# Threshold attention followed by hash routing: three start-up and routing steps moved to other places in the instruction streams

## The chip, the cores and the metric

The kernel runs on one core of a Trainium2 chip. The metric is the device time of one execution in microseconds. Before the change the median of three runs is 1003.69 us (1003.37 to 1003.96). The profile below is of one more execution, whose span is 1001.3 us.

The core has five engines that work in parallel, each through its own stream of instructions: TensorE (PE in the profile; its weight loads are PEld), VectorE (DVE), ScalarE (ACT), GpSimd (POOL) and SyncE (SP), which issues most of the DMAs.

## The reference, cut to what matters

```python
# attention: batch 8, 8 heads, 576 positions, head_dim 64
scores = (1 / np.sqrt(64)) * np.matmul(q, k.transpose(0, 1, 3, 2))
thresh = np.max(scores, axis=-1, keepdims=True) - tau
scores = np.where(scores >= thresh, scores, -1e9)
scores = scores - np.max(scores, axis=-1, keepdims=True)
attn = np.exp(scores)
attn = attn / (np.sum(attn, axis=-1, keepdims=True) + 1e-9)
x = np.matmul(attn, v)                       # (8, 8, 576, 64) -> x of (4608, 512)

# routing: 8 experts of 512 x 1024 and 1024 x 512
expert_idx = token_ids * np.int64(2654435761) % np.int64(8)
for e in range(8):
    mask = expert_idx == e
    out[mask] = np.maximum(x[mask] @ w1[e], 0.0) @ w2[e]
```

The expert of a token depends on its id alone, not on the attention. So the routing tables (which token goes to which slot of which expert) can be made while the attention runs. Each expert has 608 slots; tokens beyond that would go to an overflow list of 128-row tiles, worked off in a loop at the very end.

## The kernel before: the parts that the change touches

The attention goes over 32 pairs of heads `p`, each in five steps `s` (a step of 64 queries, then four of 128), so `n = 5 * p + s`. Step 0 has one tile of scores, the other four have two. The four operations that every tile of scores passes on its way:

```python
def score(n, j):      # PE: q times k into one of two PSUM tiles "sc"                 (line 219)
def negate(n, j):     # DVE: ns = -sc, with the row minimum; frees "sc"               (line 230)
    # behind a step's last tile, on POOL: thr = row minimum + drop                    (line 237)
def expo(n, j):       # ACT: w = exp(row minimum - ns)                                (line 244)
def mask(n, j):       # DVE: w = w * (ns <= thr), with the row sum                    (line 255)
```

Then PE transposes `w` (line 266), ACT copies the transposes out of PSUM (line 287), and PE multiplies by v (line 297). One pair later the output is normalised by DVE (`put_xm`, line 336).

The start, where tau and the identity matrix come in:

```python
load_pair(0)
...                                        # token ids, v of pair 0
load_pair(1)
make_identity(nc, ident[:])                # POOL: memset, then a select on the diagonal
none_f = a_st.tile([P, 1], FP32, name="none_f")
...                                        # memsets on DVE
with tc.manual_schedule():                 # from here in this order on every engine
    tr = ps_tr.tile([P, 2, 512], FP32, name="tr")
    for _ in range(16):
        nc.tensor.transpose(tr[:, 0, 0:P], ident[:], ident[:])      # nobody reads these
    nc.gpsimd.dma_start(out=tau_in[:], in_=...)
    nc.vector.tensor_scalar(out=keep_any[:], in0=tau_in[:], ..., op0=ALU.is_ge)
    nc.vector.tensor_scalar(out=drop[:], in0=keep_any[:], ...)
    nc.vector.tensor_tensor(out=drop[:], in0=drop[:], in1=tau_in[:], op=ALU.max)
    nc.vector.tensor_scalar(out=k_scale[:], in0=keep_any[:], ...)
    nc.vector.tensor_scalar(out=kts[0][:, 0], in0=kts[0][:, 0], scalar1=k_scale[:], ...)
    nc.scalar.activation(kts[0][:, 1], kts[0][:, 1], AF.Copy, scale=k_scale[:])
    constants()                            # iotas, memsets, triangular matrix, on POOL
    next(pieces)
    score(0, 0)
```

Routing is a generator, `route()`, cut by `yield` into pieces of at most two small DVE operations. Each `next(pieces)` puts one piece into the streams. With the calls counted from the one just above, the pieces hold:

```python
# call 3: eid, eidf            5: onehot                7, 9: two halves of a scan (incl)
# call 10: row                12: two matmuls (L407, L408) and cnt
# call 13: ot_i, twice        14: ot                   15: oend, base         16: base
# call 17: incl + base        19: incl * onehot        21: reduce to rank_f   22: rank_i
# call 23: rank_i, twice      24: rank                 25: ovt, first         26: ovt
# call 27: ovt, twice         28: first                29: slot_i, then placed.append(True)
# call 31: overflow compare   33: overflow reduce      34: min                35: two copies (ov_i)
# the calls not named (2, 4, 6, 8, 11, 18, 20, 30, 32) only reach the next yield
```

Once `placed` is set, a second generator, `scatters()`, runs one piece in each step but step 1: 36 indirect DMAs on POOL, one pair later 16 table loads on SP, one pair later two small DVE operations. From pair 26, step 2, `fetch_0` gathers rows by these tables and needs them done.

The order inside a step, cut to what matters here:

```python
for n in range(LAST + NS + 1):
    p, s = divmod(n, NS)
    ...
    if s == 3 and n < LAST:
        next(pieces, None)                 # ahead of negate(n, 0)
    ...
    if s == 1 and p + 1 < NP:
        scale_k(p + 1)                     # POOL: k of the next pair times keep_any * 0.125
    ...                                    # turns, products with v
    if n < LAST and s not in (1, 2):       # (in steps 1 and 2 this comes a little earlier)
        negate(n, 0); expo(n, 0)
    if s == 0 and n < LAST:
        next(pieces, None)                 # behind negate(n, 0), ahead of put_xm and mask
    if s == 0 and p >= 2 and n != LAST:
        put_xm(p - 2)
    ...
    score(n + 1, 0)
    negate(n, 1); expo(n, 1)
    score(n + 1, 1)
    ...
    for j in range(heads(n - 1)):
        mask(n - 1, j)
    if s != 1 and placed:
        next(scatter_pieces, None)
```

Behind this loop the tables for the experts are made (`stok`, `gidx`, `gidx_x`, on DVE), the last rows are gathered, and the first expert's matmuls go on (`fill`, line 579, each result copied out of PSUM by DVE, line 586).

Of the kernel before, what the change touches and what calls it, by code (L numbers as in the profile page):

```python
# [9 lines left out]
FP32 = mybir.dt.float32  # L10
# [4 lines left out]
ALU = mybir.AluOpType  # L15
# [5 lines left out]
def kernel(  # L21
# [12 lines left out]
    nc = tc.nc  # L34
# [51 lines left out]
    slot_i = consts.tile([P, NTC], I32, name="slot_i")  # L86
    tid32 = consts.tile([P, NTC, 2], I32, name="tid32")
    tau_in = consts.tile([P, 1], FP32, name="tau_in")
    keep_any = consts.tile([P, 1], FP32, name="keep_any")
    k_scale = consts.tile([P, 1], FP32, name="k_scale")  # L90
    drop = consts.tile([P, 1], FP32, name="drop")

# [35 lines left out]
    with tc.tile_pool(name="a_q", bufs=1) as a_q, \  # L128
# [67 lines left out]
                nc.sync.dma_start(out=v_sb[half, 4, half], in_=rows[TAIL:S, half])  # L196

        def scale_k(p):
            nc.gpsimd.tensor_scalar(out=kts[p][:], in0=kts[p][:], scalar1=keep_any[:],
                                    scalar2=SCALE, op0=ALU.mult, op1=ALU.mult)  # L200

        def heads(n):
            return 1 if n % NS == 0 else 2
# [314 lines left out]
                                      offset=0, ap=[[2 * NTC, P], [2, NTC], [1, 2]]))  # L518
        load_v(0)
        load_pair(1)  # L520
        make_identity(nc, ident[:])
        none_f = a_st.tile([P, 1], FP32, name="none_f")
        nc.vector.memset(none_f[:], 0.0)
        for w in w_bufs:
# [9 lines left out]
        def constants():  # L534

            nc.gpsimd.iota(iota_i[:], pattern=[[1, NOV]], base=0, channel_multiplier=0)
            nc.gpsimd.tensor_copy(iota_f[:], iota_i[:])
            make_upper_triangular(nc, u128[:], val=1.0, diag=False)
            nc.gpsimd.memset(ones128[:], 1.0)
            nc.gpsimd.memset(none[:], BIG)  # L540
            nc.gpsimd.memset(gidx[:], BIG)
            nc.gpsimd.memset(gidx_x[:], BIG)
            for t in sidx:
                nc.gpsimd.memset(t[:], BIG)
            nc.gpsimd.iota(tok[:], pattern=[[1, NTC]], base=0, channel_multiplier=NTC)
            for table in slot_dram:
                nc.sync.dma_start(out=table.rearrange("(p c) o -> p (c o)", p=P), in_=none[:])
# [69 lines left out]
                next(h_pieces, None)  # L617

        with tc.manual_schedule():

            tr = ps_tr.tile([P, 2, 512], FP32, name="tr")
            for _ in range(16):
                nc.tensor.transpose(tr[:, 0, 0:P], ident[:], ident[:])
            nc.gpsimd.dma_start(out=tau_in[:],
                                in_=bass.AP(tensor=tau.tensor, offset=0, ap=[[0, P], [1, 1]]))

            nc.vector.tensor_scalar(out=keep_any[:], in0=tau_in[:], scalar1=0.0, scalar2=None,
                                    op0=ALU.is_ge)  # L630
            nc.vector.tensor_scalar(out=drop[:], in0=keep_any[:], scalar1=-3e38, scalar2=3e38,
                                    op0=ALU.mult, op1=ALU.add)
            nc.vector.tensor_tensor(out=drop[:], in0=drop[:], in1=tau_in[:], op=ALU.max)
            nc.vector.tensor_scalar(out=k_scale[:], in0=keep_any[:], scalar1=SCALE, scalar2=None,
                                    op0=ALU.mult)
            nc.vector.tensor_scalar(out=kts[0][:, 0], in0=kts[0][:, 0], scalar1=k_scale[:],
                                    scalar2=None, op0=ALU.mult)
            nc.scalar.activation(kts[0][:, 1], kts[0][:, 1], AF.Copy, scale=k_scale[:])
            constants()
            next(pieces)  # L640
            score(0, 0)
            for n in range(LAST + NS + 1):
                p, s = divmod(n, NS)
                m = n - 2
                if s == 0 and p + 2 < NP:
                    load_pair(p + 2)
                if s == 0 and p + 1 < NP:
                    load_v(p + 1)
                if s == 2 and p in (20, 24):
                    load_w1(p // 4 - 5)  # L650
                if s == 2 and p in (22, 26):
                    load_w2((p - 22) // 4)

                if s == 3 and n < LAST:
                    next(pieces, None)
                if s == 1 and 3 <= p < 2 + KT:
                    nc.sync.dma_start(out=xg_bufs[p - 2][:], in_=xg_bufs[0][:])

                if s == 1 and 2 + KT <= p < 2 + KT + N // DIN:
                    r0 = DIN * (p - 2 - KT)  # L660
                    nc.sync.dma_start(
                        out=x_dram[r0:r0 + DIN, DIN - P:].rearrange("(t p) m -> p t m", p=P),
                        in_=xg_bufs[0][:].rearrange("p (t m) -> p t m", m=P))
                q = p - 1
                if s == 1 and 0 <= q < NP:
                    add_eps(q)
                if s == 1 and p + 1 < NP:
                    scale_k(p + 1)
                if s == 2 and 0 <= q < NP:
                    nc.vector.reciprocal(recs[q][:], recs[q][:])  # L670
                if n == LAST + NS:
                    fill(2)
                if s == 0 and p >= 2:
                    turn_o()
                if n == LAST:
                    for k in (0, 2):
                        tr = ps_sc.tile([P, 2, 512], FP32, name="sc")
                        early_xT(tr, k, k + 2, 0, CO - 1)
                if s in (1, 2) and 0 <= q < NP and n != LAST + 1:
                    av_part(q, 0, ((0, 1, 2), (3, 4))[s - 1])  # L680
                if n < LAST and s in (1, 2):
                    negate(n, 0)
                    expo(n, 0)
                if s == 2 and 0 <= q < NP:
                    put_oT(0)
                if n > LAST:
                    fill(1)
                turned = 0 <= m < LAST
                if turned:
                    tr = turn_w(m, 0)  # L690
                    put_wT(m, 0, tr)
                if n == LAST:
                    put_xm(p - 2)
                    av_part(q, 0, (0, 1, 2))
                if n >= LAST:
                    fill(1)
                if n == LAST:
                    tr = ps_sc.tile([P, 2, 512], FP32, name="sc")
                    early_xT(tr, 4, 5, 0, CO - 1)
                if s in (3, 4) and 0 <= q < NP:  # L700
                    av_part(q, 1, ((0, 1, 2), (3, 4))[s - 3])
                if n < LAST and s not in (1, 2):
                    negate(n, 0)
                    expo(n, 0)
                if s == 0 and n < LAST:
                    next(pieces, None)
                if s == 0 and p >= 2 and n != LAST:
                    put_xm(p - 2)
                if s == 4 and 0 <= q < NP:
                    put_oT(1)  # L710
                if s in (3, 4) and turned:
                    tr = turn_w(m, 1)
                if n + 1 < LAST:
                    score(n + 1, 0)
                if s == 4 and turned:
                    put_wT(m, 1, tr)
                if n < LAST and heads(n) == 2:
                    negate(n, 1)
                    expo(n, 1)
                if s == 3 and turned:  # L720
                    put_wT(m, 1, tr)
                if n + 1 < LAST:
                    score(n + 1, 1)
                if s in (0, 1) and turned:
                    tr = turn_w(m, 1)
                    put_wT(m, 1, tr)
                if 0 < n <= LAST:
# [6 lines that stand above are left out]
                if n >= G0 and s > 1 and early:  # L734
                    assert routed
                    fetch_0(*early.pop(0))
                if n == LAST:
                    fill(1)
            assert not early
            nc.vector.tensor_tensor(out=stok[:], in0=stok[:], in1=stok_odd[:], op=ALU.min)  # L740
            for h in range(4):
                rows, n = slice(32 * h, 32 * h + 32), (NB - h + 3) // 4
                nc.vector.tensor_copy(gidx[rows, :, 0:n], stok[rows, :, h::4])
            for g in range(4):
                rows, n = slice(32 * g, 32 * g + 32), min(KT, NB - KT * g)
                nc.vector.tensor_copy(gidx_x[rows, 1:, 0:n], stok[rows, 1:, KT * g:KT * g + n])
            for kt in range(KT):
                fetch_0(kt, HP - 1)
            fill(FO * 2 * (CO - 1) - 18)
            tr = ps_tr.tile([P, 2, 512], FP32, name="tr")  # L750
            early_xT(tr, 0, KT, CO - 1, CO)
# [195 lines left out]
```

## Time and profile before

| engine | busy us | share of the span |
|---|---|---|
| PE | 983.8 | 98% |
| DVE | 517.7 | 52% |
| ACT | 436.9 | 44% |
| POOL | 291.7 | 29% |

The shares are averages over two stages. In the attention (to about 455 us) PE and DVE are both busy nine tenths of the time or more; in the experts' stage (from about 475 us) PE alone is. A pair takes about 13.9 us in the steady part of the attention.

The start, in the order of the trace: POOL writes zeros for the identity at 0.90 us, issues tau's DMA at 1.48 us (0.74 us of POOL's time), and makes the diagonal at 2.32 us. PE's 16 transposes run from 2.69 us; the last starts at 5.95 us. DVE starts `keep_any` at 4.65 us, which ends a wait of 1.41 us for tau's transfer, the two operations of `drop` at 4.83 and 5.02 us, `k_scale` at 5.10 us, and the first scaling of k at 5.28 us. The first scores start at 6.30 us, the first `negate` at 7.60 us.

In the lists by group, "x32" is the number of instructions, and the number behind the comma is the mean duration of one in ns. In the timeline, the first two columns are the start and the duration in us; what stands in brackets is the idle time of the engine before the instruction and what ended it.

### The profile page before, as it was taken

The page shows a single profiled execution, that of the slowest core. Times are in us where ns is not written, and L with a number is a line of the kernel's source. Part 1 is how long each engine was busy: PE and PEld are TensorE (multiplying, and loading weights), DVE is VectorE, ACT ScalarE, POOL GpSimd, SP SyncE. Part 2 cuts the span into 40 slices and gives each one's busy share as a digit, 9 for nine tenths or more (in the row PEclk, how much of TensorE's full clock was granted, in tenths as well). Part 3 has the DMA queues.
Part 4 walks back from the last instruction along what each step waited for, and adds up shares of the span by engine and source line. Part 5 has one row for each costly group of instructions (what it writes and reads, how often), then busy time and mean ns, then how long its engine had stood idle before and what let it go on. Part 6 is the DMA issues. An engine that isn't in the chain of part 4 may idle for free.

```text
span 1001.3 us, 20487 instructions
## 1 busy us (share of the span) xinstructions
PE 983.8 (98%) x7562; PEld 653.9 (65%) x7562; DVE 517.7 (52%) x1378; ACT 436.9 (44%) x714; POOL 291.7 (29%) x413
## 2 busy tenths in 40 slices
PE   7999999999999999999999999999999999999995
PEld 4666666666666666666766857768578577685773
DVE  7999999999999999994311010010101100200000
ACT  5988888888988889883200000010010000100000
POOL 3233323377676335550321030030210300300101
PEclk9999999999999999999999999999999999999998
DMA  7355544564467677410166344272352533801001
GB/s 182 74 129 141 129 117 112 136 141 107 92 185 169 154 195 194 114 49 25 39 189 185 116 105 143 91 211 89 106 163 84 158 91 104 222 1 39 27 10 57
DMA packets 145779, 117.07 MB, mean 117 GB/s; under 512 B 59860, under 2 KB 120280, under 8 KB 145680
## 3 DMA queue, kind: packets, MB, share of 16 engines
q1 hardware_dynamic: 135408, 96.41, 37.9%
q0 software_dynamic: 7824, 18.91, 6.1%
q8 instruction: 61, 1.00, 0.4%
q10 hardware_dynamic: 2448, 0.44, 0.2%
q14 instruction: 38, 0.31, 0.1%
HBM read 81.99 MB, written 22.37 MB: 104 GB/s over the span
## 4 chain that ended last, share of the span: by engine, by line
PE 87%; issue 6%; SPq 2%; DMA 2%; ACT 1%; DVE 1%; POOL 0%; POOLq 0%; ACTq 0%
PE sc L784 20%; PE av L297 17%; PE sc L219 15%; PE o_ps L802 12%; PE tr L266 10%; PE sc L815 8%; PE sc L579 3%; SPq L835 2%; PE av L266 1%; DMA out_dram<-o_last,gidx 1%; DMA out_dram<-o,gidx 1%; ACT w L244 1%; PE xT_ps L596 0%; PE sc L596 0%; ACT wT_a L287 0%
## 5 line engine op out<-in xcount | busy, mean ns | idle before, releaser
L244 ACT ACTIVATE w<-ns,nmx 128x576 f32<-128x576 f32 x288 | 220.3, 776 | 33.2 <-DVE ns L230 33.1
L784 PE MATMUL sc<-xT,w_sb 128*128 128x304 f32 x896 | 230.4, 419 | 0.0
L255 DVE SCALAR_TENSOR_TENSOR w<-ns,thr,w 128x576 f32<-128x576 f32 x288 | 225.4, 814 | 0.4 <-POOL thr L237 0.4
L784 PEld LDWEIGHTS sc<-xT,w_sb 128*128 128x128 f32 x896 | 170.2, 190 | 61.4 <-issue 3.3
L230 DVE TENSOR_SCALAR_CACHE_REDUCE ns<-sc 128x576 f32<-128x576 f32 x288 | 205.2, 744 | 6.3 <-PE sc L219 5.6
L219 PE MATMUL sc<-k_sb,q 64*128 64x288 f32 (+1 forms) x1280 | 179.2, 426 | 0.6 <-DVE ns L230 0.4
L802 PE MATMUL o_ps<-w_sb,h 128*128 128x512 f32 (+2 forms) x400 | 166.2, 575 | 0.0
L266 PEld LDWEIGHTS tr<-ident,w 64*128 64x128 f32 x2624 | 106.6, 139 | 88.7 <-ACT wT_b L287 26.3
L237 POOL TENSOR_SCALAR thr<-nmx,drop 128x2 f32<-128x2 f32 (+1 forms) x160 | 101.8, 637 | 176.7 <-DVE ns L230 163.4
L792 DVE TENSOR_SCALAR h<-sc 128x608 f32<-128x608 f32 x28 | 22.2, 791 | 240.9 <-PE sc L784 240.9
L266 PE MATMUL tr<-ident,w 64*128 64x64 f32 x2624 | 139.3, 231 | 2.7 <-ACT wT_a L287 2.0
L804 ACT COPY o<-o_ps 128x512 f32<-128x512 f32 (+2 forms) x25 | 14.2, 569 | 274.5 <-PE o_ps L802 248.1
L802 PEld LDWEIGHTS o_ps<-w_sb,h 128*128 128x128 f32 x400 | 74.9, 190 | 86.8 <-issue 84.7
L841 POOL DMA_INDIRECT out_dram<-o,gidx x24 | 23.9, 996 | 324.0 <-ACT o L804 291.4
L219 PEld LDWEIGHTS sc<-k_sb,q 64*128 64x128 f32 (+1 forms) x1280 | 93.0, 179 | 22.9 <-DVE ns L230 9.7
L297 PE MATMUL av<-wT_a,v 128*64 128x320 f32 (+1 forms) x704 | 100.4, 418 | 0.0
L790 ACT ACTIVATE h<-sc 128x608 f32<-128x608 f32 x28 | 19.0, 677 | 182.0 <-PE sc L784 182.0
L815 PE MATMUL sc<-h,w_sb 128*128 128x224 f32 x512 | 98.2, 352 | 0.0
L815 PEld LDWEIGHTS sc<-h,w_sb 128*128 128x128 f32 x512 | 96.9, 190 | 1.1
L287 ACT COPY wT_a<-tr 128x512 f32<-128x512 f32 (+1 forms) x128 | 81.7, 638 | 20.7 <-PE tr L266 20.1
L287 ACT COPY wT_b<-tr 128x512 f32<-128x512 f32 (+1 forms) x128 | 81.2, 634 | 6.4 <-PE tr L266 4.0
L297 PE MATMUL av<-wT_b,v 128*64 128x256 f32 x640 | 83.2, 389 | 0.0
(118 smaller groups left out, 547.9 us busy)
## 6 DMA issues: line engine op xcount, KB each, us to landing
w_sb<-in_moe_w_dram SPq DMA_DIRECT2D x16, 2048.0 KB
q<-in_q_dram SPq DMA_DIRECT2D x62, 288.0 KB
v<-in_v_dram SPq DMA_DIRECT2D x32, 256.0 KB
x_scratch<-xm SPq DMA_DIRECT2D x32, 256.0 KB
xT<-xq SPq DMA_DIRECT2D x84, 80.0 KB
k_sb<-in_k_dram SPq DMA_DIRECT2D x31, 144.0 KB
k_sb<-in_k_dram SPq DMA_DIRECT2D x32, 112.0 KB
o_last<-oq SPq DMA_DIRECT2D x210, 16.0 KB
```

The lines of the kernel that those rows point to most:

```text
L219: nc.tensor.matmul(sc[out_rows, i, 0:S2], lhsT=q_sb[rows, h, q0:q1], rhs=k_sb[rows, h], start=True, stop=True)
L230: nc.vector.tensor_scalar(out=ns[:].rearrange("p (i s) -> p i s", i=2), in0=sc[:, :, 0:S2], scalar1=-1.0, scalar2=None, op0=ALU.mult, op1= ...
L237: nc.gpsimd.tensor_scalar(out=thr[:, 0:j + 1], in0=stats[n][0][:, 0:j + 1], scalar1=drop[:], scalar2=None, op0=ALU.add)
L244: nc.scalar.activation(w, nss[n, j][:], AF.Exp, bias=stats[n][0][:, j:j + 1], scale=-1.0)
L255: nc.vector.scalar_tensor_tensor(out=w, in0=nss.pop((n, j))[:], scalar=stats[n][1][:, j:j + 1], in1=w, op0=ALU.is_le, op1=ALU.mult, accum_ ...
L266: nc.tensor.transpose(dst[:, r, 64 * c:64 * c + 64], src[rows, c0:c0 + P], ident[rows, rows])
L287: nc.scalar.copy(dst, tr[:, :, 0:64 * n_c].rearrange("p r (c q) -> p r c q", c=n_c))
L297: nc.tensor.matmul(av[64 * j:64 * j + 64, g, c0:c1], lhsT=v_sb[:, c, 64 * j:64 * j + 64], rhs=wT[g][:, i, c0:c1], start=(c == 0), stop=stop)
L579: nc.tensor.matmul(h_ps[:, i, 0:CH], lhsT=w1_sb[:, co, fo * P:fo * P + P], rhs=xT_0[:, co, i * CH:i * CH + CH], start=(co == 0), stop=(co ...
L784: nc.tensor.matmul(h_ps[:, i, 0:width], lhsT=w1_sb[:, co, fo * P:fo * P + P], rhs=xT[:, co, i * width:i * width + width], start=(co == 0), ...
L802: nc.tensor.matmul(o_ps[:, 0:width], lhsT=h_sb[:, fo, FIRST[kt]:FIRST[kt] + P], rhs=w2_sb[:, fo, cols], start=(fo == 0), stop=(fo == FO - 1))
L815: nc.tensor.matmul(oT_ps[:, i, c * OW:c * OW + OW], lhsT=w2_sb[:, fo, co * P:co * P + P], rhs=h_sb[:, fo, FIRST[KF]:CAP], start=(fo == ord ...
```

## The change

It has three parts. First, the identity is made at the head of the fixed order, ahead of tau's transfer on POOL, and one transpose more is run on it. Second, `keep_any` goes: `k_scale` is worked out of tau in one operation, and `drop` is worked out behind the first scaling of k; `scale_k` then multiplies by one scalar and not by two. Between tau's landing and the first scaling of k there is then one operation on DVE where there were four. Third, routing starts later (in step 3 of pair 1, then step 0 of pair 2, where it was step 0 and step 3 of pair 0), and it stops being called once `placed` is set. What is left of it, the overflow list, is put behind the attention's loop.

```diff
-    keep_any = consts.tile([P, 1], FP32, name="keep_any")
 ...
         def scale_k(p):
-            nc.gpsimd.tensor_scalar(out=kts[p][:], in0=kts[p][:], scalar1=keep_any[:],
-                                    scalar2=SCALE, op0=ALU.mult, op1=ALU.mult)
+            nc.gpsimd.tensor_scalar(out=kts[p][:], in0=kts[p][:], scalar1=k_scale[:],
+                                    scalar2=None, op0=ALU.mult)
 ...
         load_pair(1)
-        make_identity(nc, ident[:])
 ...
         with tc.manual_schedule():
+            make_identity(nc, ident[:])
             tr = ps_tr.tile([P, 2, 512], FP32, name="tr")
-            for _ in range(16):
+            for _ in range(17):
                 nc.tensor.transpose(tr[:, 0, 0:P], ident[:], ident[:])
             nc.gpsimd.dma_start(out=tau_in[:], ...)
-            nc.vector.tensor_scalar(out=keep_any[:], in0=tau_in[:], scalar1=0.0, scalar2=None,
-                                    op0=ALU.is_ge)
-            nc.vector.tensor_scalar(out=drop[:], in0=keep_any[:], scalar1=-3e38, scalar2=3e38,
-                                    op0=ALU.mult, op1=ALU.add)
-            nc.vector.tensor_tensor(out=drop[:], in0=drop[:], in1=tau_in[:], op=ALU.max)
-            nc.vector.tensor_scalar(out=k_scale[:], in0=keep_any[:], scalar1=SCALE, scalar2=None,
-                                    op0=ALU.mult)
+            nc.vector.tensor_scalar(out=k_scale[:], in0=tau_in[:], scalar1=0.0, scalar2=SCALE,
+                                    op0=ALU.is_ge, op1=ALU.mult)
             nc.vector.tensor_scalar(out=kts[0][:, 0], in0=kts[0][:, 0], scalar1=k_scale[:],
                                     scalar2=None, op0=ALU.mult)
             nc.scalar.activation(kts[0][:, 1], kts[0][:, 1], AF.Copy, scale=k_scale[:])
+            nc.vector.tensor_scalar(out=drop[:], in0=tau_in[:], scalar1=0.0, scalar2=3e38,
+                                    op0=ALU.is_lt, op1=ALU.mult)
+            nc.vector.tensor_tensor(out=drop[:], in0=drop[:], in1=tau_in[:], op=ALU.max)
 ...
-                if s == 3 and n < LAST:
-                    next(pieces, None)
+                if s == 3 and p > 0 and not placed:
+                    next(pieces)
 ...
-                if s == 0 and n < LAST:
-                    next(pieces, None)
+                if s == 0 and p > 1 and not placed:
+                    next(pieces)
 ...
                 nc.vector.tensor_copy(gidx_x[rows, 1:, 0:n], stok[...])
+            for _ in pieces:
+                pass
             for kt in range(KT):
                 fetch_0(kt, HP - 1)
```

## The prediction

> **What bounds the kernel now.** I read the chain of work that ended last first. Its shares by engine:
>
> ```profile
> PE 87%; issue 6%; SPq 2%; DMA 2%; ACT 1%; DVE 1%; POOL 0%; POOLq 0%; ACTq 0%
> ```
>
> PE sets the time almost everywhere, so work that leaves another engine counts only where PE waits for it. The change touches three places: the first 20 us, the attention's loop, and its end. I looked at each for itself. The start, from the timeline:
>
> ```profile
> 11.64 0.75 POOL L199 TENSOR_SCALAR k_sb<-k_sb,keep_any 128x576 f32<-128x576 f32 x1 [2.86 <-DMA k_sb<-in_k_dram]
> ...
> 12.37 0.58 POOL L237 TENSOR_SCALAR thr<-nmx,drop 128x2 f32<-128x2 f32 x2
> 12.71 0.82 DVE L255 SCALAR_TENSOR_TENSOR w<-ns,thr,w 128x576 f32<-128x576 f32 x1 [0.40 <-POOL thr L237]
> ...
> 14.20 0.18 DVE L380 TENSOR_SCALAR eid<-tid 128x36 int32<-128x36 int32 x1
> 14.40 0.18 DVE L382 CAST eidf<-eid 128x36 f32<-128x36 int32 x1
> 14.50 0.75 DVE L230 TENSOR_SCALAR_CACHE_REDUCE ns<-sc 128x576 f32<-128x576 f32 x1
> ```
>
> The reader is to see that POOL scales pair 1's k only when its DMA has landed, that thr of step 1 stands behind that, and that DVE then waits 0.40 us for thr. This DMA is issued by SP, which does not wait for tau. From 12.71 us on DVE has no gap up to 20.2 us, and the routing piece `eid` stands in the middle of it. The chain in order of time has it too:
>
> ```profile
> 12.39 0.30 POOL thr L237
> 12.69 0.03 issue
> 12.71 1.56 DVE w L255 x4
> 14.28 0.10 DVE eid L380
> ```
>
> For the loop I took the starts of `put_xm` (line 336) as pair marks: pair 2 at 35.51 us, pair 17 at 246.13 us, then 13.89 to 13.91 us a pair. Busy times by stretch, in the columns PE, PEld, DVE, ACT, POOL, granted clock:
>
> ```profile
> 63.42:77.64 14.22, 14.22 (x178) 8.98 (x176) 13.91 (x41) 12.51 (x21) 4.50 (x9) 1.00 0.53 132
> ...
> 105.80:119.73 13.93, 13.93 (x176) 8.79 (x174) 13.93 (x42) 12.23 (x20) 4.40 (x8) 1.00 0.50 121
> ...
> 147.89:162.15 14.26, 14.16 (x177) 8.71 (x174) 13.99 (x42) 12.15 (x21) 4.41 (x8) 1.00 0.47 116
> ...
> 260.04:273.94 13.90, 13.90 (x176) 8.81 (x176) 13.84 (x41) 12.28 (x21) 9.92 (x13) 1.00 0.47 107
> ```
>
> PE has no idle time in 13.90 us, DVE almost none: the two are nearly matched. So where in a pair a DVE piece stands decides what it costs. The step after step 0 shows it. This is a pair without routing:
>
> ```profile
> 291.54 0.31 PEld L219 LDWEIGHTS sc<-k_sb,q 64*128 64x128 f32 x4 [0.17 <-DVE ns L230]
> ```
>
> The scores of step 2 wait for the PSUM tile that `negate` of step 1 frees. Behind `negate` of step 0, which itself waits for PE, DVE has `put_xm`, two masks and two negates before that point, and they fill the time. Now the same scores in the chain, in pair 3 without a piece in step 0 and in pair 4 with the smallest one (`row`, 63.34 to 63.42 us):
>
> ```profile
> 52.86 1.03 PE sc L219 x8
> ...
> 66.76 1.10 PE sc L219 x8
> ```
>
> A delay of 0.08 us on DVE became 0.07 us on PE. There is no slack here.
>
> [...] `eid` delays the negate behind it. [...] the stretch 18.75 to 22.10 us is granted 0.50, and step 0's eight score matmuls take 1.24 us there (from 19.13 us) against 0.71 us at 300.27 us. [...] the trace has 0.09 us (155.10 to 155.19) and 0.37 us (28.54 to 28.91) from start to start. [...]
>
> **The change part by part.**
>
> Identity and tau. POOL's select took 0.32 us and would now stand ahead of tau's DMA. I let tau land 0.35 us later (4.65 becomes 5.00). The chain from there to the first scaling of k was 5.28 - 4.65 = 0.63 us for four operations; with one it is 5.28 - 5.10 = 0.18 us. Scaling starts at 5.18 us, 0.10 us earlier. The transposes start about 1 us earlier (ready at about 1.7 us), and with 17 of them at 0.213 us they no longer stand in front of the first scores, which may move from 6.30 to some 5.8 us[...]. But all of this runs into the wait at 12.71 us, which hangs on pair 1's k. I count 0.05 us gain, from whatever one scalar fewer saves in POOL's 0.75 us.
>
> Routing out of pair 0. `eid` and `eidf` hold DVE from 14.20 to 14.50 us on the chain: minus 0.30 us.
>
> Routing in the loop. Before, the pair marks from pair 2 to pair 17 take 210.62 us, against 15 x 13.90 = 208.50: routing costs 2.12 us there, though its DVE time is near 7 us. The reason is the place. Counting calls, step 3 gets the odd ones before, and there stand the long pieces; the periods with only a 0.37 us piece in step 3 are 13.93 and 13.92 us (calls 17 and 19): almost free, since DVE has some 0.35 us of slack there. Step 0 gets the even ones: 0.08 to 0.11 us each, or nothing; their periods show 0.09 to 0.10 us more (calls 10, 14, 26, 28).
>
> The change turns this round. Call 2 falls in step 3 of pair 1, call 3 in step 0 of pair 2, so every odd call now stands in step 0, ahead of `put_xm`. Their start-to-start times in the trace: call 3 0.30; calls 5, 7, 9, 17, 19 0.37 each, 1.85; calls 13 and 15 0.28 each, 0.56; call 21 0.59; calls 23 and 25 0.18 each, 0.36; call 27 0.33; call 29 0.11. The sum is 4.10 us, and by the `row` line nearly all of it goes through to PE. The even calls move to step 3 and become free, except call 12: its two matmuls take 0.14 us of PE itself, and with the wait for them I put it at 0.20 us (it cost 0.32 before). The loop then has 4.30 us in place of 2.12: plus 2.18 us. The overflow pieces (calls 31 to 35), which leave the loop, are within the 2.12; pairs 15 to 17 show 0.12, 0.22 and 0.05 us.
>
> The scatters start at step 0 of pair 15 and not at step 3 of pair 13. Their last DVE pieces come to pair 26: one of about 0.09 us in step 0 (plus 0.09), one in step 2 (nothing). The table loads come to pair 25, behind a w1 load that lands at about 358.7 us, as its 4096-byte packets show; the tables are wanted near 371 us. I count no wait.
>
> The end of the attention. The overflow list takes 0.34 + 0.33 + 0.09 + 0.27 = 1.03 us on DVE. It comes between these two groups of work:
>
> ```profile
> 475.40 0.73 DVE L586 COPY h<-sc 128x608 f32<-128x608 f32 x1
> ...
> 476.29 0.91 DVE L769 MEMSET o_last<- 128x1024 f32 x1 [0.16 <-issue]
> 477.13 1.01 POOL L110 DMA_INDIRECT xg<-x_scratch,gidx  x1 [0.30 <-issue]
> 477.41 0.79 DVE L586 COPY h<-sc 128x608 f32<-128x608 f32 x1 [0.20 <-PE sc L579]
> ```
>
> The first copy would end at 476.13 + 1.03 = 477.16 us; PE wants its PSUM tile at about 477.36, where the next tile is done and DVE's next copy starts. It just fits. I count plus 0.15 us.
>
> Sum: -0.05 - 0.30 + 2.18 + 0.09 + 0.15 = +2.07 us. No trace shows a piece of 0.37 us in step 0, and a part of such a delay may be hidden; I take 0.5 us off. Predicted: 1003.69 + 1.6 = 1005.3 us.
>
> **The rivals.** First: routing's cost is its DVE time wherever it stands. Then the change is pure gain: 0.30 for `eid`, 0.39 for the overflow pieces, 0.05 at the start, so 1003.0 us. For it speaks that DVE is busy 13.9 of 13.9 us; against it that calls 17 and 19, of 0.37 us each, cost 0.03 and 0.02 us. Second: the start is worth more than I think, because [...] the half-clock stretch at 18.75 us goes. That stretch would give up to some 1 us (half of what PE must do in 3.35 us, less its idle part). Against it: pair 1's k lands when it lands, and between 8.50 and 18.60 us PE was busy 7.00 of 10.10 us because DVE fed it, which does not change. It would make 1004.3 us with my loop, or 1002.0 with the first rival's. Third: a new wait, for the tables at pair 26 or in the copies at the end, of 1 to 3 us: 1006 to 1008 us.
>
> **Range and chances.** My mechanism alone gives 1004.8 to 1006.2 us, depending on how much of 4.10 us shows. The first two rivals widen it downward, the third upward. The range is 1003.2 to 1006.8 us. All of this is under 0.5%, so a change of 2% either way has a chance of one in a hundred.
>
> **What would show it.** In the changed profile: `eid` in step 0 of pair 2 and DVE free of it at 14.2 us; DVE's idle time ahead of the first mask of step 1 grown from 0.40 us and that mask still near 12.7 us; pair marks from pair 2 to 15 with periods up to 14.3 us where a long piece stands in step 0, and step 2's scores in the chain at 1.03 us plus the piece; 13.90 us from pair 16 on. Wrong would be: periods near 13.9 us with long pieces in step 0; a first mask well before 12.7 us; PE idle behind the copies at 475 us.

## The result and the profile after

| kernel | median us | from to |
|---|---|---|
| before | 1003.66 | 1002.43 to 1004.46 (6 runs) |
| changed | 1011.45 | 1009.61 to 1013.19 (6 runs) |

The changed kernel is 7.8 us slower: the ratio is 1.0078, with a 95% interval of 1.0065 to 1.0091. The direction was predicted, the size was not (1.6 us, with 3.1 us as the upper end of the range).

The chain of work that ended last, shares by engine, is nearly what it was. So the loss is many small waits and not a new bound:

```profile
PE 86%; issue 6%; SPq 2%; DMA 2%; DVE 1%; ACT 1%; POOL 0%; POOLq 0%; DVEq 0%; ACTq 0%
```

The starts of `put_xm` on DVE serve as pair marks again. They show where the 6.6 us between the two spans (1001.3 and 1007.9 us) come in:

| mark | before | after | difference | grown since the last row |
|---|---|---|---|---|
| pair 2 | 35.51 | 35.96 | 0.45 | 0.45, of which 0.31 is `eid`, now just ahead of this mark |
| pair 17 | 246.13 | 249.35 | 3.22 | 2.77 |
| pair 26 | 371.27 | 374.66 | 3.39 | 0.17 |
| pair 28 | 399.23 | 404.96 | 5.73 | 2.34 |
| the last | 471.32 | 477.03 | 5.71 | 0 |
| span | 1001.3 | 1007.9 | 6.6 | 0.9 |

The first row is to be read with care: in three profiles in which the instructions up to this mark are those of the kernel before, it lies at 34.69, 35.51 and 36.15 us. The rows of the loop repeat far better: from mark 2 to mark 14 no period of the changed kernel differs by over 0.02 us between its two profiles.

**The start.** The list by group has POOL's scaling of k, a group of 31. First the kernel before, then the changed one (busy time in us and mean ns behind the bar):

```profile
L199 POOL TENSOR_SCALAR k_sb<-k_sb,keep_any 128x576 f32<-128x576 f32 x31 | 23.1, 746 | 5.7 <-DMA k_sb<-in_k_dram 2.9
```

```profile
L198 POOL TENSOR_SCALAR k_sb<-k_sb,k_scale 128x576 f32<-128x576 f32 x31 | 53.8, 1734 | 6.9 <-DMA k_sb<-in_k_dram 4.1
```

The same elements, with one multiplication in place of two, take 1.73 us in place of 0.75. The timeline of the changed kernel shows what waits for it:

```profile
11.84 1.75 POOL L198 TENSOR_SCALAR k_sb<-k_sb,k_scale 128x576 f32<-128x576 f32 x1 [4.10 <-DMA k_sb<-in_k_dram]
...
13.57 0.58 POOL L236 TENSOR_SCALAR thr<-nmx,drop 128x2 f32<-128x2 f32 x2
13.91 0.82 DVE L254 SCALAR_TENSOR_TENSOR w<-ns,thr,w 128x576 f32<-128x576 f32 x1 [2.87 <-POOL thr L236]
```

The first scores are earlier (5.67 us, before 6.30), but the first mask of step 1 is later (13.91 us, before 12.71). DVE idles 2.87 us ahead of it, and PE 3.03 us behind it.

**The loop.** Pair 4 in the timeline, with half of the scan now in step 0:

```profile
64.14 0.45 DVE L392 TENSOR_TENSOR_SCAN incl<-keep,onehot 128x144 f32<-128x144 f32 x1
64.51 0.80 DVE L335 TENSOR_TENSOR xm<-av,rec 128x640 f32<-128x640 f32 x1
```

The scores of step 2 behind it, in the chain in order of time, are 0.32 us longer than the 1.03 us of a free pair:

```profile
67.59 1.35 PE sc L218 x8
```

The matching stretches, with the columns of before, show that PE counts as busy during this wait (from mark 3 to mark 4, with the half scan ahead of mark 4; and a stretch without routing, from mark 18 to mark 19):

```profile
50.24:64.51 14.27, 14.27 (x178) 8.88 (x176) 14.08 (x41) 12.28 (x21) 5.02 (x9) 1.00 0.49 124
...
263.26:277.17 13.91, 13.91 (x176) 8.83 (x176) 13.82 (x41) 12.29 (x21) 10.00 (x13) 1.00 0.46 108
```

Call 12 fell in step 3 of pair 6, where DVE now waits for its matmuls:

```profile
100.44 0.17 DVE L409 COPY cnt<-av 128x16 f32<-128x16 f32 x1 [0.50 <-PE av L407]
```

**Pairs 26 to 28.** The stretches from mark to mark take 14.92 and 15.38 us; before they took 13.90 and 14.06 us:

```profile
374.66:389.58 14.92, 14.70 (x178) 8.96 (x176) 13.90 (x43) 12.94 (x22) 6.87 (x10) 1.00 0.85 234
389.58:404.96 15.38, 14.54 (x174) 8.85 (x174) 13.73 (x39) 12.47 (x20) 8.08 (x11) 1.00 0.68 158
```

The waits of DVE between these marks have one large entry (total us, times, longest), and the timeline shows the second of the two:

```profile
DVE w L254 <- POOL thr L236: 2.3, 2, 1.4
```

```profile
401.32 1.09 POOL L109 DMA_INDIRECT xg<-x_scratch,gidx  x1 [5.04 <-DVE ns L229]
402.47 0.30 POOL L236 TENSOR_SCALAR thr<-nmx,drop 128x2 f32<-128x2 f32 x1
402.80 0.82 DVE L254 SCALAR_TENSOR_TENSOR w<-ns,thr,w 128x576 f32<-128x576 f32 x1 [1.39 <-POOL thr L236]
```

A gather stands ahead of thr in POOL's queue. The profile names DVE as the releaser of the gather, but what it waited for were late stores of x, whose rows it reads: in the trace, the semaphore of the last of three stores fires at 400.56 us, and POOL's wait for it ends at 400.58 us. For the first gather of pair 26, at 385.92 us, these two times are 385.00 and 385.03 us. In the kernel before, the profile itself names the stores as what this gather waited for (the semaphore fires at 378.00 us):

```profile
378.93 1.13 POOL L110 DMA_INDIRECT xg<-x_scratch,gidx  x1 [0.94 <-DMA x_scratch<-xm]
```

That is 7.7 us behind the mark of pair 26; in the changed kernel it is 11.3 us. SP's own timeline shows the stores of pair 24 and the w2 load behind them:

```profile
380.05 0.54 SPq L341 DMA_DIRECT2D x_scratch<-xm  x1
380.64 1.15 SPq L346 DMA_DIRECT2D x_scratch<-xm  x2
381.83 0.59 SPq L124 DMA_DIRECT2D w_sb<-in_moe_w_dram  x1
```

The w2 load goes out 7.2 us behind the mark of pair 26; before it was 4.7 us (376.0 against 371.3). Ahead of these, SP spent 365.9 to 374.7 us on the 16 table loads. The next stores are later still, 8.2 us behind the mark of pair 27 (before 5.4): ahead of them SP waited 3.2 us at the loads of v, where its own waits name the w2 load, and 3.4 us at the first store, where they name a gather.

**The end.** A copy on DVE now ends behind the overflow list and a memset, and PE waits for it:

```profile
482.06 0.91 DVE L768 MEMSET o_last<- 128x1024 f32 x1 [0.16 <-issue]
482.92 1.48 DVE L584 COPY h<-sc 128x608 f32<-128x608 f32 x2
483.75 8.45 PE L577 MATMUL sc<-xT,w_sb 128*128 128x304 f32 x32 [0.67 <-DVE h L584]
```

The memset of `o_last` stood behind the first copy before (476.29 against 475.40 us) and stands ahead of it now.

So there were four candidates: the slow scaling, the long pieces in step 0, the table loads, and the overflow list. The rival was that the slow scaling, in POOL's queue ahead of thr and the gathers, is behind most of it.

### The profile page after: what moved, and what is told of

Read it like the earlier page. It is cut to its first block, busy times and chain, and to the rows that moved or that the text cites. A ratio compares the mean times of both kernels' runs of the same rounds, so it can differ in the third digit from the quotient of the medians.

```text
span 1007.9 us, 20494 instructions
## 1 busy us (share of the span) xinstructions
PE 987.4 (98%) x7563; PEld 655.4 (65%) x7563; DVE 519.3 (52%) x1377; ACT 437.5 (43%) x714; POOL 306.1 (30%) x413
## 4 chain that ended last, share of the span: by engine, by line
PE 86%; issue 6%; SPq 2%; DMA 2%; DVE 1%; ACT 1%; POOL 0%; POOLq 0%; DVEq 0%; ACTq 0%
PE sc L783 19%; PE av L296 17%; PE sc L218 15%; PE o_ps L801 12%; PE tr L265 10%; PE sc L814 8%; PE sc L577 2%; SPq L834 2%; PE av L265 1%; DMA out_dram<-o_last,gidx 1%; DMA out_dram<-o,gidx 1%; PE xT_ps L594 0%; ACT w L243 0%; PE sc L594 0%; ACT wT_a L286 0%
## 5 line engine op out<-in xcount | busy, mean ns | idle before, releaser
L236 POOL TENSOR_SCALAR thr<-nmx,drop 128x2 f32<-128x2 f32 (+1 forms) x160 | 86.7, 542 | 158.6 <-DVE ns L229 150.0
L803 ACT COPY o<-o_ps 128x512 f32<-128x512 f32 (+2 forms) x25 | 14.2, 569 | 274.5 <-PE o_ps L801 248.0
```

Source lines behind the costliest of these rows:

```text
L236: nc.gpsimd.tensor_scalar(out=thr[:, 0:j + 1], in0=stats[n][0][:, 0:j + 1], scalar1=drop[:], scalar2=None, op0=ALU.add)
```

## The experiments

Every ratio is to the kernel before on the same chip. The experiments ran on three chips, on which the kernel before has medians of 1007.62, 1003.62 and 1008.41 us. On the first and the third, pairs 14 to 31 of all kernels are less regular than in the two profiles above (on the first, the period up to mark 17 of the kernel with the overflow list late is 14.49 us, that of the changed kernel above 13.90), so periods there are compared with care. The changed kernel ran on the chip of the result and on the third chip (ratios 1.0078 and 1.0077), not on the first; what came back on the first is worked out from the ratios.

### One loss at a time taken out of the changed kernel

**Two operations in the scaling.**

```diff
-  nc.gpsimd.tensor_scalar(..., scalar1=k_scale[:], scalar2=None, op0=ALU.mult)
+  nc.gpsimd.tensor_scalar(..., scalar1=k_scale[:], scalar2=1.0, op0=ALU.mult, op1=ALU.mult)
```

> The changed kernel with POOL's scaling of k written with two operations again (times k_scale, times 1.0). In the changed kernel this instruction takes 1.73 us with one operation, in the kernel before 0.75 us with two. Theory A (four separate losses that add up: slow scaling, long pieces in step 0, tables, overflow list): the instruction is back at 0.75 us, the first mask of step 1 moves from 13.9 us to about 12.9 us and about 1.0 us of the 7.8 us comes back; pairs 2 to 16 stay as slow as in the changed kernel (14.3 us where a 0.37 us piece stands in step 0). Rival B (the slow scaling in POOL's queue is behind most of the loss, since thr and the gathers stand behind it): 4 us or more comes back, in the loop and at pairs 27 and 28.

The instruction is back at 0.745 us and the first mask of step 1 is at 12.99 us. The ratio is 1.0065 (1.0053 to 1.0077). The changed kernel itself was 1.0078 and, on the third chip, 1.0077, so some 1.3 us came back, though the intervals overlap. The periods from mark 2 to mark 15 are those of the changed kernel to 0.02 us, and the two long ones stay (15.27 and 15.84 us). The rival falls.

**Long pieces back in step 3.**

```diff
             nc.gpsimd.memset(ones_e[:], 1.0)
             yield
-            yield
 ...
-                if s != 1 and placed:
+                if s != 1 and placed and n >= 75:
```

> The changed kernel with one yield fewer at the head of the routing, so that the long pieces fall in step 3 again; the scatters are held to the same step as in the changed kernel (step 0 of pair 15). Theory A (the step decides what a piece costs): pairs 2 to 16 lose about 1 us in all against 13.90 us a pair where the changed kernel loses 4, so the kernel gains some 2.5 us on the changed one; start, pairs 27 and 28 and the end are unchanged. Rival C (a piece costs its DVE time in any step): no gain, 0 us.

The ratio is 1.0045 (1.0033 to 1.0058), 3.3 us less than the changed kernel's. From mark 2 to mark 16 it takes 196.13 us, the changed kernel 199.49, the kernel before 196.67. The DVE instructions are the same ones. The stretch from mark 3 to mark 4, with half of the scan in step 3 (58.66 us), is:

```profile
51.45:65.36 13.91, 13.91 (x176) 8.79 (x176) 13.91 (x42) 12.27 (x21) 4.95 (x8) 1.00 0.50 127
```

Rival C falls: 0.37 us of DVE cost nothing here and 0.37 us in step 0. The two long periods stay (14.12 and 16.03 us).

**Tables one pair earlier.**

```diff
-            for _ in range(4):
-                yield
             for table, dst in zip(slot_dram, sidx):
```

> The changed kernel with the table loads one pair earlier (pair 24, step 0: the four empty pieces behind the last scatter are left out), as are the two DVE pieces that use them. Theory A (16 table loads on SP at pair 25 push back the stores of x, and the first gather waits for these on POOL): the periods of 14.9 and 15.4 us at pairs 26 to 28 go back to 13.9 to 14.1 us, 2.3 us or more comes back. Rival D (the gathers are late because of the w2 load of pair 26 or of the slow scaling on POOL): the two long periods stay, under 0.7 us comes back.

The ratio is 1.0055 (1.0042 to 1.0068), 2.3 us less than the changed kernel's. The intervals overlap slightly. The first long period went (13.95 us), the second did not (15.31 us). So it was run again beside the changed kernel:

> The changed kernel with the table loads one pair earlier, run beside the changed kernel itself. Theory A: both long periods between pairs 26 and 28 shrink, that of pairs 26 to 27 to 13.9 us, the next to 14.5 us or less (what the slow scaling leaves), and about 1.9 us comes back. Rival: the second long period stays above 15 us.

> The changed kernel as it is, to be compared on one chip with the others of this call. 0.7 to 0.9% slower than the kernel before; the start at half clock for one window or for three, and the mark of pair 2 near 36 us or near 38 us accordingly.

A window is 3.41 us here, the time at a granted clock of 0.50 in the profiles of both kernels (18.71 to 22.13 us before, 15.75 to 19.16 us in the changed one).

The ratios are 1.0059 (1.0045 to 1.0073) and 1.0077 (1.0063 to 1.0091): 1.9 us came back, with intervals that overlap. But in the profile of this second run the periods are 15.30 and 16.10 us, no shorter than those of the changed kernel beside it (14.16 and 16.21). Here the tables meet another large load: w1 goes out behind them, at 364.2 us, in the changed kernel beside it at 355.2. SP then stands at two loads of v for 7.89 us, and the next stores of x go out at 376.8 to 379.6 us, over 21 us behind the ones before. In the first run's profile SP stands there for 6.27 us. So the edit moves the collision by a pair and does not remove it. Where the 1.9 us came back is not shown: the execution profiled was the slowest of the five (1016.10 us), that of the changed kernel the second fastest of its five (1015.02 us).

**Overflow list behind the copies.**

```diff
-            for _ in pieces:
-                pass
             for kt in range(KT):
                 fetch_0(kt, HP - 1)
             fill(FO * 2 * (CO - 1) - 18)
+            for _ in pieces:
+                pass
```

> The changed kernel with the overflow list one place later, behind the copies of the first expert's results and not ahead of them. Theory A (the list's operations on DVE hold up a copy that PE waits for): PE's idle time of 0.67 us behind that copy goes and about 0.9 us comes back, all of it behind 477 us. Rival E (the end is longer for another cause, the memsets or the gathers): no gain, 0 us.

The ratio is 1.0069 (1.0056 to 1.0082), 0.9 us less than the changed kernel's, with overlapping intervals. The traces are plainer: PE has no wait of over 0.1 us there any more. In the six profiles with the list ahead of the copies, the time from the last mark to the end is 530.6 to 531.0 us; in the seven others that end alike (without the kernel with the added POOL instructions, below) it is 529.7 to 530.0 us. The same copies in the timeline, the second now waiting for PE and not PE for it:

```profile
487.10 0.73 DVE L584 COPY h<-sc 128x608 f32<-128x608 f32 x1
487.99 0.91 DVE L768 MEMSET o_last<- 128x1024 f32 x1 [0.16 <-issue]
489.11 0.79 DVE L584 COPY h<-sc 128x608 f32<-128x608 f32 x1 [0.20 <-PE sc L577]
```

The memset of `o_last` has gone back behind the first copy too. This run does not part what the list costs from what the memset costs.

### One part at a time put into the kernel before

**The slow scaling alone.**

```diff
-  scalar1=keep_any[:], scalar2=SCALE, op0=ALU.mult, op1=ALU.mult
+  scalar1=k_scale[:], scalar2=None, op0=ALU.mult
```

> The kernel before with one edit: POOL scales k by k_scale in one operation, as in the changed kernel. Theory A: the instruction goes from 0.75 us to 1.73 us, the first mask of step 1 waits some 1 us longer for thr (12.7 us becomes 13.7 us), PE idles longer there and is at half clock for one to three windows of 3.4 us afterwards; the steady loop is unchanged. 1 to 3 us slower. Rival B (thr behind the slow scaling holds every pair back): 31 pairs times some tenths, 5 us or more.

The ratio is 1.0015 (1.0008 to 1.0022): 1.0 us in the medians (1004.62 against 1003.62). The scaling takes 1.73 us, the first mask comes at 13.79 us, and pairs 3 to 26 keep the periods of before. Only the period from pair 27 to 28 grows (14.50 us, before 14.06). So about 1 us, not 31 times some tenths.

**The first part of the change alone, with the scaling in two operations.**

> The kernel before with the first part of the change alone: identity ahead of tau's transfer, 17 transposes, k_scale in one operation, drop behind the scaling of k; POOL's scaling of k keeps two operations (k_scale, 1.0). Theory A: the first scores start 0.6 us earlier, but the first mask of step 1 stays at 12.7 to 13.0 us since it hangs on the transfer of pair 1's k; no gain, within 0.5 us of the kernel before. Rival F (the earlier start carries through, as the change meant): 0.6 us or more faster.

The edit is the first part of the change's diff, with scalar2=1.0 in the scaling. The ratio is 1.0004 (0.9996 to 1.0013): no gain. The timeline shows why:

```profile
11.54 0.75 POOL L198 TENSOR_SCALAR k_sb<-k_sb,k_scale 128x576 f32<-128x576 f32 x1 [3.39 <-DMA k_sb<-in_k_dram]
12.27 0.58 POOL L236 TENSOR_SCALAR thr<-nmx,drop 128x2 f32<-128x2 f32 x2
12.61 0.82 DVE L254 SCALAR_TENSOR_TENSOR w<-ns,thr,w 128x576 f32<-128x576 f32 x1 [1.15 <-POOL thr L236]
```

The earlier scores end in a longer wait at the same place, 12.61 us, for pair 1's k.

**The tables at pair 25 alone.**

```diff
-            for _ in range(4):
+            for _ in range(10):
                 yield
             for table, dst in zip(slot_dram, sidx):
```

> The kernel before with one edit: six more empty pieces ahead of the table loads, so that they stand at pair 25, step 0, as in the changed kernel; scaling, routing and overflow list are those of before. Theory A (the 16 loads hold SP for 8 us, so the stores of x and the w2 load behind them go out 2 to 4 us late, and the gathers of pairs 26 and 27 with them): periods of 14.5 us or more twice between pairs 26 and 28, 1.5 to 2.5 us slower. Rival (it takes the slow scaling on POOL as well): under 0.5 us slower.

The ratio is 1.0014 (1.0006 to 1.0021). The profile has both long periods, 15.17 and 15.71 us, with the same entry among DVE's waits:

```profile
DVE w L255 <- POOL thr L237: 2.9, 2, 1.7
```

w2 goes out 7.2 us behind the mark of pair 26, as in the changed kernel. So neither the slow scaling nor the pieces' places are needed for this loss. Its size in the medians, 1.3 us, is less than the 2.9 us by which these periods exceed those of the first table; what the kernel before loses there on this chip was not profiled. The last kernel below ran on this chip too, with its tables at pair 23: its two periods are 14.29 and 14.03 us, and DVE has no wait for thr. The first gather of pair 26 starts 7.4 us behind the mark there and 11.5 us behind it here.

**The forms of POOL's instruction, behind the last store of the kernel before.**

> The kernel before with ten more POOL instructions behind its last store, on 128 x 512 f32 in SBUF, for their durations alone: times a column, times a column and times 1.0, times a constant, times a column twice, plus a column, each twice, then a copy. Theory A (any one-operation form is slow): the forms with one operation take about 1.54 us (1.73 x 512 / 576), those with two about 0.67 us. Rival H (only the multiplication by a column alone is slow): the plus and the constant take 0.67 us too.

Four of the five forms in the timeline, in this order: times a column; times a column and times 1.0; times a constant; times a column twice:

```profile
994.64 1.60 POOL L893 TENSOR_SCALAR xg<-xg,k_scale 128x512 f32<-128x512 f32 x1
...
996.21 0.70 POOL L893 TENSOR_SCALAR xg<-xg,k_scale 128x512 f32<-128x512 f32 x1
996.88 1.49 POOL L893 TENSOR_SCALAR xg<-xg 128x512 f32<-128x512 f32 x1
...
998.36 0.75 POOL L893 TENSOR_SCALAR xg<-xg,k_scale 128x512 f32<-128x512 f32 x1
```

The fifth, plus a column, took 1.57 us, and the second round repeats all of them to 0.05 us. Rival H falls: in these five forms it is the number of operations, not the multiplication and not the column. DVE and ACT had no work of their own from 991 to 1004 us (in the kernel before, with the same instructions on both, the last one ends at 990.24 us), so these times, 1.48 to 1.60 us with one operation among them, stand without any work of theirs.

### All losses taken out

**All four edits in the changed kernel** (the scaling, one `yield` fewer, the four empty pieces left out, the list behind the copies; the scatters not held back, so that the tables are loaded at pair 23 as in the kernel before).

> The changed kernel with all four suspected losses taken out: two operations in the scaling of k, long pieces back in step 3, tables loaded at pair 23 as in the kernel before, overflow list behind the copies. Theory A: the whole 0.8% comes back, and what is left is the gain of routing out of pair 0 (0.3 us) and of the overflow list out of the loop (0.4 us): 0.0 to 1.0 us faster than the kernel before. Rival G (the change holds a further loss that is not named yet): 1 us or more slower than the kernel before.

1001.71 us, ratio 0.9989 (0.9982 to 0.9996): slightly faster than the kernel before. The periods from pair 26 are 13.91 and 14.07 us, and DVE has no wait for thr there. Nothing large is left unnamed: singly, the four edits gave back 1.3, 3.3, 1.9 to 2.3 and 0.9 us, 7.4 to 7.8 us of the 7.8.

**The same with pair 1's k loaded earlier.** The start still hung on that transfer, so one more edit:

```diff
         load_pair(0)
+        load_pair(1)
         nc.sync.dma_start(out=tid32[:], ...)
         load_v(0)
-        load_pair(1)
```

> The kernel with all four losses taken out, with the loads of pair 1 put ahead of the token ids and of v of pair 0 on SP. Theory A (the start hangs on the transfer of pair 1's k, not on tau): POOL's scaling of pair 1 starts about 2 us earlier than at 11.6 us, the first mask of step 1 comes at about 11.4 us as soon as DVE is free, and the kernel is 0.5 to 1.5 us faster than without this edit. Rival (the start hangs on something else, such as DVE or the half clock): no gain from this edit, 0.1 to 0.2% faster than the kernel before as without it.

1006.06 us against 1008.41, ratio 0.9977 (0.9969 to 0.9986): the lowest ratio of all here. It was not run beside the kernel without this edit; across the two chips the ratios differ by 0.12%, some 1.2 us, and their intervals overlap. Its start:

```profile
9.38 1.04 POOL L198 TENSOR_SCALAR k_sb<-k_sb,k_scale 128x576 f32<-128x576 f32 x1 [1.52 <-DMA k_sb<-in_k_dram]
...
10.41 0.30 POOL L236 TENSOR_SCALAR thr<-nmx,drop 128x2 f32<-128x2 f32 x1
...
11.09 0.81 DVE L254 SCALAR_TENSOR_TENSOR w<-ns,thr,w 128x576 f32<-128x576 f32 x1
```

The mask has no bracket: DVE comes to it without a wait, and pair 2's mark is at 32.68 us, 2.0 to 3.5 us earlier than in the three profiles with the start of before.

### The half clock at the start

The time to pair 2's mark goes mainly with the length of a stretch at half clock (granted 0.50): 34.47 to 36.05 us with 3.4 us of it, 36.55 to 38.07 us with 10.2. All profiles, with PE's idle time ahead of step 1's transposes:

| kernel | PE's wait there, us | at half clock, us | mark of pair 2 |
|---|---|---|---|
| before | 0.6 | 3.4 | 35.51 |
| before, POOL's instructions added at the end | 0.8 | 3.4 | 34.69 |
| before, tables at pair 25 | 1.5 | 6.8 | 36.15 |
| slow scaling alone | 1.6 | 3.4 | 35.69 |
| first part alone | 1.3 | 10.2 | 36.55 |
| changed | 3.0 | 3.4 | 35.96 |
| changed, again | 2.5 | 10.2 | 37.52 |
| two operations in the scaling | 1.9 | 3.4 | 36.05 |
| long pieces in step 3 | 2.6 | 10.2 | 37.52 |
| tables one pair earlier | 2.9 | 10.2 | 37.98 |
| tables one pair earlier, again | 2.3 | 10.2 | 37.55 |
| overflow list late | 3.0 | 10.2 | 38.07 |
| all losses out | 1.9 | 3.4 | 34.47 |
| and pair 1 earlier | none | 0 | 32.68 |

The stretch of half clock in the changed kernel's second profile, and the same time in the last kernel:

```profile
13.70:23.90 10.20, 7.78 (x66) 5.42 (x68) 9.13 (x25) 6.44 (x10) 2.56 (x5) 0.50 0.72 164
```

```profile
6.10:24.10 18.00, 15.15 (x162) 8.26 (x158) 17.10 (x48) 13.91 (x21) 6.62 (x11) 1.00 0.93 208
```

The stretches are 3.4, 6.8 and 10.2 us long, so one, two and three times 3.4. The length of PE's wait does not decide this: 3.0 us had 3.4 us at half clock behind it in one profile and 10.2 in another, and 1.3 us had 10.2. In four profiles in which both were read, the place where the half clock begins goes with its length. With 10.2 us, it begins at about 13.7 us in the changed kernel's second profile, ahead of the wait's end at 14.76, and at about 13.9 us with the first part alone, 0.3 us behind the wait's end at 13.58. With 3.4 us, it begins at 15.75 us in the changed kernel's first profile, 0.9 us behind the wait's end at 14.88, and at 18.71 us before, 5.0 us behind the wait's end at 13.68. The same kernel had 3.4 us in one execution and 10.2 us in another, and its mark of pair 2 then lies 1.6 us later (35.96 against 37.52, on two chips). This may be why the median of the changed kernel lies above the 1009.61 us of the execution profiled first. All this is read across profiles; no run set the length by itself, and what brings the half clock about is not shown.

## Why the prediction was wrong, step by step

Of the 6.6 us between the two profiles, the loop up to mark 17 with `eid` makes 3.1 us (counted: 2.2, less 0.5), pairs 26 to 28 make 2.3 (counted: 0.1), the end 0.9 (counted: 0.15), and the start 0.1 (counted: a gain of 0.35); 0.2 more lie between marks 17 and 26. The start's part is within what it varies by.

**Identity and tau: this step failed on POOL's cost.** The step said that one scalar fewer saves something of POOL's 0.75 us and counted a gain of 0.05 us. The instruction went to 1.73 us. The wait at 12.71 us was foreseen as the place where an earlier start would end, and it was; what stands ahead of it got longer. Undoing it brought back some 1.3 us; alone it costs 1.0 us.

**Routing out of pair 0: not told apart.** `eid` left the chain at 14.2 us, but its 0.30 us cannot be told from the rest of the start.

**Routing in the loop: right mechanism, terms too small.** The step said 4.30 us in place of 2.12. From mark 2 to mark 17 the changed kernel takes 213.39 us, against 15 x 13.90 = 208.50: 4.89 us, and with `eid`'s 0.31 us ahead of mark 2 it is 5.20 us. Single pieces of 0.37 us from start to start (`onehot` on 128x288 f32, the halves of the scan on 128x144) cost what was said (the periods that end at marks 3, 4 and 5 are 14.28, 14.27 and 14.25 us, so 0.38, 0.37 and 0.35). Three terms were mis-sized. Call 12 was put at 0.20 us; in step 3, DVE waited 0.50 us for its matmuls, and of the 0.86 us of its period 0.45 are left for it when call 13's 0.41 are taken off. Call 21 took its 0.59 us on DVE, but the period that ends with it is 14.77 us, 0.87 over 13.90; DVE waits 0.26 us for scores at the end of this period, and why is open. And three pieces of two operations took longer ahead of `put_xm` than in their old place: calls 13 and 15 0.41 us each from start to start where 0.28 was read off, call 27 0.43 where 0.33 was (call 23, also two operations, took 0.18 us in both places). The 0.5 us that was taken off for hidden delays should not have been: nothing was hidden. That the place of the pieces is the cause is shown by the run with the long pieces back in step 3.

**Tables at pair 25: this step failed.** "I count no wait" looked at when the tables are wanted, and that was right: they came in time. It did not look at what stands behind them on SP. The 16 loads took SP 8.8 us, the stores of x and w2 went out 2.5 us late, the gathers waited for those stores, and thr stood behind the gathers. That made 2.34 us in the profile, 1.3 us in the medians of the run that did this alone. That the place of the table loads is the cause is shown by that run; the way from SP to thr is read off the traces. The third rival named "a new wait, for the tables at pair 26 or in the copies at the end": at pair 26 it was a new wait, but not for the tables; in the copies it was right.

**The end: this step was mis-sized.** It said that the list just fits and counted 0.15 us. It took 0.9 us. The copy came at 482.92 us, 5.9 us behind `put_xm`; in the kernel before that was 4.1 us (475.40 and 471.32). The list accounts for about 1.0 us of these 1.8, as was said; the rest is the memset of `o_last`, which now stands ahead of the copy (0.83 us from start to start and an idle 0.16 us ahead of it). By an estimate from these times, the copy would have ended at about 482.7 us without the memset, and PE stopped at 483.08 us: the list alone would just have fitted. The step did not foresee that the memset would change its place.

**The rivals.** The first, that place does not matter, fell with the run that only moved the pieces. The second, that the start is worth more than counted, was right that the half clock goes with the time of the start (the marks of pair 2 above) and wrong about the sign. That its stretch would go was the author's estimate: in the changed kernel it lasted 3.4 us in one profile and 10.2 us in the other, 3.4 us before, and it was gone only in the one profile in which pair 1's k came earlier.

## What to carry to other kernels

In a loop in which two engines are nearly matched (here PE is busy 13.90 us and DVE 13.84 us of 13.90), ask of every small operation which wait it stands ahead of: 0.37 us of DVE cost 0.00 us in one step and 0.37 us in another of the same pair. A batch of DMA issues that is itself in time can still be late for what stands behind it in the same queue: here 16 issues took SP 8.8 us, and the w2 load behind them went out 7.2 us behind its mark in place of 4.7. And an earlier start is worth only what the next wait lets through: here the wait on the next pair's k swallowed all of it (ratio 1.0004 for the first part of the change alone), while moving that load took the wait away (the mask at 11.09 us, without a wait ahead of it).

## What the runs showed of the hardware that was not expected

On POOL, a tensor-scalar instruction with one operation was slower in these runs than with two: 1.73 us against 0.75 us on 128 x 576 f32, and on 128 x 512 f32 1.56 to 1.60 (times a column), 1.48 to 1.49 (times a constant) and 1.57 (plus a column) against 0.68 to 0.75 us. A second operation that does nothing (times 1.0) made it more than twice as fast, 0.745 us in place of 1.73 in the changed kernel. No run tells why.
